# Strassen-Winograd products in the feed-forward part of an adaLN transformer block, with its normalised rows transposed through DRAM

## The chip, the cores and the metric

The kernel runs on 1 core of one Trainium2 chip. The metric is device time in microseconds (us): the median over executions of one kernel. A profiled execution also gives a span, from its first to its last recorded instruction; the timer reads 1.7 to 1.8 us more than the span of the same execution.

In what follows PE is TensorE (matmuls), VectorE is DVE, ScalarE is ACT, GpSimd is POOL, and SP is the engine whose queue issues most loads.

## The reference

A block of a conditioned transformer on x of 2048 tokens by D = 1024, all in bf16. Six modulation rows come from `c` and `w_mod`. A linear-attention half with its own projection `wo` comes first; the change leaves it alone except for its last stretch. Then comes a gated feed-forward part (FFN) with F = 3584:

```python
h = _layernorm(x, axis=-1) * (1 + ca) + sa
x = x + ga * _A_ref(h, A_wqkv, A_wo)                 # linear attention, then @ wo
h = _layernorm(x, axis=-1) * (1 + cb) + sb           # LN2
x = x + gb * ((_gelu(h @ w_gate) * (h @ w_up)) @ w_down)   # 1024 -> 3584 -> 1024
```

## The kernel before

The tokens are handled in 4 groups of 512 (`TG`). The residual x stays in SBUF, the core's on-chip memory (`xres`). The attention half ends with the products by `Wo`; there each finished 128x512 tile in PSUM, the memory that the matmuls write (`psw`, two buffers), is scaled, added to `xres`, and LN2 follows. LN2 transposes its rows on PE:

```python
def wo_proj(tg, oT):
    for tl in range(TT):
        for half in range(NHD):
            psw = psWO.tile([P, NW], FP32, name="psw", tag="wo")      # psWO has bufs=2
            for g in range(KD):
                nc.tensor.matmul(psw[:], lhsT=oT[:, g, tl * P:(tl + 1) * P],
                                 rhs=Wo_sb[:, g, half * NW:(half + 1) * NW], ...)
            gated_residual_update(psw, xres[tt], half, garow)         # two VectorE instructions

def ln_finish(tg, xhs, hT, opc, scol0, ps_pool, pstag):
    for tl, xh in enumerate(xhs):
        psxh = ps_pool.tile([P, D], BF16, name="psxh", tag=pstag)
        for kd in range(KD):
            nc.tensor.transpose(psxh[:, kd * P:(kd + 1) * P], xh[:, kd * P:(kd + 1) * P], ident[:])
        nc.scalar.activation(out=hT[:, :, tl * P:(tl + 1) * P], in_=psxh..., func=AF.Copy)
    # ... scale and shift on VectorE
```

The FFN runs group by group. Every 128 columns of F take 8 matmuls for the gate, 8 for up, and a chain of five instructions on ScalarE and VectorE that makes the gelu and the product. The down product then takes 8 tiles of 28 matmuls:

```python
for jf ...:                                             # 28 per group of tokens
    for k in range(KD): nc.tensor.matmul(psg[:], lhsT=wg_t[...], rhs=h2T[:, k, :], ...)
    for k in range(KD): nc.tensor.matmul(psu[:], lhsT=wu_t[...], rhs=h2T[:, k, :], ...)
    nc.scalar.activation(out=tsq[:], in_=psg[:], func=AF.Square, scale=SQRT_A)
    nc.vector.scalar_tensor_tensor(out=w[:], in0=tsq[:], scalar=1.0, in1=psg[:], ...)
    nc.scalar.activation(out=s[:], in_=w[:], func=AF.Sigmoid, scale=SIG_SCALE)
    nc.vector.tensor_tensor(out=gl[:], in0=s[:], in1=psg[:], op=ALU.mult)
    nc.vector.tensor_tensor(out=actT[:, jf, :], in0=gl[:], in1=psu[:], op=ALU.mult)
...
for tl ...:
    for half ...:
        for jf in range(JF): nc.tensor.matmul(psdn[:], lhsT=actT[...], rhs=wd_sb[...], ...)
        gated_residual_update(psdn, xres[tt], half, gbrow)
```

A tile allocated with a `tag` from a pool takes turns with the other tiles of that tag over the pool's `bufs` buffers; a new tile waits until the old one in its buffer is done with. The framework's scheduler decides in which order each engine gets its instructions, from the program's order and priorities.

## Time and profile before

| | before |
|---|---|
| median, 16 runs | 889.22 us (887.97 to 892.59) |
| span of the profiled execution | 887.5 us |
| PE busy | 97% |
| VectorE, ScalarE busy | 59%, 33% |
| FFN matmuls (gate, up, down) | 2688 |

The page of the profile gives the busy time of each engine (share of the span, number of instructions), the chain of work that ended last by engine, and the costliest groups of instructions (line, engine, operation, output and inputs, shapes, count; then busy us, mean ns of one; then idle time before them).

```profile
PE 859.2 (97%) x4224; PEld 397.7 (45%) x4224; DVE 522.2 (59%) x1015; ACT 294.7 (33%) x518; POOL 3.4 (0%) x27
PE 79%; DVE 10%; DMA 4%; ACT 2%; issue 2%; SPq 1%; ACTq 0%
L409 PE MATMUL psg<-h2T,wg_t 128*128 128x512 bf16 x896 | 211.8, 379 | 0.6 <-DVE gl L423 0.6
L413 PE MATMUL psu<-h2T,wu_t 128*128 128x512 bf16 x896 | 211.7, 379 | 0.0
L432 PE MATMUL psdn<-wd_sb,actT 128*128 128x512 bf16 x896 | 194.9, 379 | 0.0
L424 DVE TENSOR_TENSOR actT<-gl,psu 128x512 bf16<-128x512 bf16 x112 | 77.0, 687 | 12.6 <-DVE gl L423 1.4
```

PE is the limit, and it hardly waits: 0.6 us of idle time in front of 2688 FFN matmuls. The mean of 379 ns is the duration of one matmul in the pipeline, not its price; the price is the distance between starts. PE's timeline gives that (start us, duration us, then the group). In the next fence, 8 psu matmuls start at 832.89 and the next group starts at 834.62, so 8 cost 1.73 us, and one costs 216 ns.

```profile
831.16 1.89 PE L409 MATMUL psg<-h2T,wg_t 128*128 128x512 bf16 x8
832.89 1.89 PE L413 MATMUL psu<-h2T,wu_t 128*128 128x512 bf16 x8
834.62 48.51 PE L432 MATMUL psdn<-wd_sb,actT 128*128 128x512 bf16 x224
```

The next fence is the view by windows of the same kernel: first the Wo stretch, then the FFN. Each line has start:end, the length, then the busy time of PE, weight loads, VectorE, ScalarE and GpSimd with instruction counts in brackets, PE's granted clock, the busy share of the DMA engines, and GB/s.

```profile
222.86:299.16 76.30, 73.72 (x374) 33.33 (x373) 73.50 (x158) 43.11 (x86) 0.00 (x0) 1.00 0.18 56
299.16:883.10 583.94, 583.15 (x2746) 265.86 (x2744) 275.90 (x427) 150.61 (x240) 0.00 (x0) 1.00 0.35 113
```

In the Wo stretch both PE and VectorE are busy for nearly all of the 76 us. In the FFN stretch VectorE is busy for less than half. The 2681 FFN matmuls in this stretch (7 had run earlier) at 215.8 ns are 578.6 us of its 583.9 us. Another 3.6 us are 64 of the LN2 transposes. 16 of them begin at 299.16, and the next matmul at 300.05.

```profile
299.16 1.06 PE L207 MATMUL psxh<-ident,xh 128*128 128x128 bf16 x16
300.05 0.38 PE L409 MATMUL psg<-h2T,wg_t 128*128 128x512 bf16 x1
```

So the FFN has about 1.8 us of idle time and hardly any slack: to shorten it, PE must be given less to do.

### The profile page before, as it was taken

What the parts mean: (1) busy time and instruction counts of PE and PEld (TensorE: products, weight loads), DVE (VectorE), ACT (ScalarE), POOL (GpSimd) and SP (SyncE); (2) the same over time, 40 slices, a digit from 0 to 9 for tenths busy, and PEclk for the clock granted to TensorE, in tenths of its full rate; (3) what the DMA queues carried; (4) which work ended last, traced back from release to release, by engine and by line L of the source; (5) the groups of instructions that cost most, each with busy time, mean ns of one, the idle gap of its engine ahead of it and who ended that gap; (6) DMA issues with size and microseconds to landing.
All of it is one profiled execution on the core that took longest, in us unless ns stands there. A gap on an engine that the chain in (4) does not pass through costs nothing.

```text
span 887.5 us, 10672 instructions
## 1 busy us (share of the span) xinstructions
PE 859.2 (97%) x4224; PEld 397.7 (45%) x4224; DVE 522.2 (59%) x1015; ACT 294.7 (33%) x518; POOL 3.4 (0%) x27
## 2 busy tenths in 40 slices
PE   5898999999999999999999999999999999999998
PEld 3354444444444444444444444444444444444443
DVE  5699978657899865562255655225656214565411
ACT  3255362527665433340023333003333002333200
POOL 0000000000000000000000000000000000000000
PEclk9999999999999999999999999999999999999999
DMA  9944044020500493541033544003544301453000
GB/s 307 353 111 96 1 96 95 13 84 0 190 1 1 159 347 113 187 141 63 24 97 108 186 144 142 24 24 103 182 151 134 107 24 54 149 181 105 1 24 24
DMA packets 107954, 96.37 MB, mean 109 GB/s; under 512 B 34560, under 2 KB 96000, under 8 KB 107904
## 3 DMA queue, kind: packets, MB, share of 16 engines
q1 hardware_dynamic: 105600, 91.49, 33.1%
q10 hardware_dynamic: 2304, 4.20, 1.3%
q8 instruction: 33, 0.54, 0.3%
q14 instruction: 17, 0.14, 0.0%
HBM read 83.10 MB, written 4.19 MB: 98 GB/s over the span
## 4 chain that ended last, share of the span: by engine, by line
PE 79%; DVE 10%; DMA 4%; ACT 2%; issue 2%; SPq 1%; ACTq 0%
PE psdn L432 21%; PE psg L409 21%; PE psu L413 21%; PE pskv L268 8%; PE psq L300 3%; DVE bnst L180 2%; DMA wmt<-in_w_mod_dram 2%; PE psw L351 2%; DMA wqkv<-in_A_wqkv_dram 2%; DVE rt L342 1%; DVE wmt L157 1%; SPq L134 1%; DVE xres L343 1%; PE kvzps L280 1%; DVE xh L195 1%
## 5 line engine op out<-in xcount | busy, mean ns | idle before, releaser
L409 PE MATMUL psg<-h2T,wg_t 128*128 128x512 bf16 x896 | 211.8, 379 | 0.6 <-DVE gl L423 0.6
L413 PE MATMUL psu<-h2T,wu_t 128*128 128x512 bf16 x896 | 211.7, 379 | 0.0
L432 PE MATMUL psdn<-wd_sb,actT 128*128 128x512 bf16 x896 | 194.9, 379 | 0.0
L416 ACT ACTIVATE tsq<-psg 128x512 bf16<-128x512 f32 x112 | 66.8, 597 | 300.9 <-PE psg L409 300.2
L409 PEld LDWEIGHTS <-wg_t 128*128 128x128 bf16 x896 | 87.7, 98 | 106.1 <-issue 0.8
L413 PEld LDWEIGHTS <-wu_t 128*128 128x128 bf16 x896 | 87.7, 98 | 105.6
L432 PEld LDWEIGHTS <-actT 128*128 128x128 bf16 x896 | 87.6, 98 | 105.0
L423 DVE TENSOR_TENSOR gl<-gs,psg 128x512 bf16<-128x512 bf16 x112 | 76.9, 687 | 78.7 <-ACT gs L421 78.6
L268 PE MATMUL pskv<-wqkv,h1T 128*128 128x512 bf16 x512 | 118.4, 386 | 3.9 <-DMA wqkv<-in_A_wqkv_dram 3.9
L418 DVE SCALAR_TENSOR_TENSOR gw<-tsq,psg 128x512 bf16<-128x512 bf16 x112 | 77.0, 688 | 66.4 <-ACT tsq L416 66.4
L342 DVE TENSOR_TENSOR rt<-psdn,gbrow 128x512 bf16<-128x512 f32 x32 | 22.1, 692 | 146.4 <-PE psdn L432 146.4
L421 ACT ACTIVATE gs<-gw 128x512 bf16<-128x512 bf16 x112 | 70.5, 630 | 83.9 <-DVE gw L418 83.9
L424 DVE TENSOR_TENSOR actT<-gl,psu 128x512 bf16<-128x512 bf16 x112 | 77.0, 687 | 12.6 <-DVE gl L423 1.4
L268 PEld LDWEIGHTS <-h1T 128*128 128x128 bf16 x512 | 49.6, 99 | 59.9 <-issue 3.5
L351 PE MATMUL psw<-wo_sb,oT 128*128 128x512 bf16 x256 | 61.5, 379 | 0.2 <-DVE rt L342 0.2
L300 PE MATMUL psq<-h1T,wqkv 128*128 128x512 bf16 x256 | 57.8, 379 | 0.0
L180 DVE BATCH_NORM_STATS2 bnst<-xres 128x6 f32<-128x512 bf16 x64 | 41.9, 672 | 5.2 <-DMA xres<-in_A_x_dram 5.1
L221 ACT ACTIVATE phie<-pskv 128x512 bf16<-128x512 f32 x32 | 19.2, 600 | 72.8 <-PE pskv L268 52.2
L157 DVE CUSTOM_DVE_ANT_0 wmt<-wmt,srow 128x1024 bf16<-128x1024 bf16 x32 | 39.2, 1226 | 2.4 <-DMA wmt<-in_w_mod_dram 2.4
L351 PEld LDWEIGHTS <-oT 128*128 128x128 bf16 x256 | 24.9, 98 | 32.1 <-issue 4.6
L300 PEld LDWEIGHTS <-wqkv 128*128 128x128 bf16 x256 | 24.7, 98 | 28.3
L224 DVE TENSOR_SCALAR phie<-phie 128x512 bf16<-128x512 bf16 x64 | 18.6, 293 | 18.7 <-ACT phie L221 18.7
(69 smaller groups left out, 465.1 us busy)
## 6 DMA issues: line engine op xcount, KB each, us to landing
wg_t<-in_B_w_gate_dram SPq DMA_DIRECT2D x28, 1024.0 KB, 5.4
wu_t<-in_B_w_up_dram SPq DMA_DIRECT2D x28, 1024.0 KB, 7.4
wd_sb<-in_B_w_down_dram SPq DMA_DIRECT2D x7, 1024.0 KB, 11.2
wqkv<-in_A_wqkv_dram SPq DMA_DIRECT2D x3, 2048.0 KB, 17.4
xres<-in_A_x_dram SPq DMA_DIRECT2D x16, 256.0 KB, 6.4
wmb<-in_w_mod_dram SPq DMA_DIRECT2D x4, 1024.0 KB, 11.3
out_dram<-xres ACTq DMA_DIRECT2D x16, 256.0 KB, 2.0
wo_sb<-in_A_wo_dram SPq DMA_DIRECT2D x1, 2048.0 KB, 8.2
```

Of the source, the lines that this page charges most:

```text
L180: nc.vector.bn_stats(out=stats[:, cb, :], in_=xt[:, cb * BW:(cb + 1) * BW])
L268: nc.tensor.matmul(ps[:], lhsT=h1T[:, k, tl * P:(tl + 1) * P], rhs=Wqkv_sb[:, k, col0:col0 + NW], start=(k == 0), stop=(k == KD - 1))
L300: nc.tensor.matmul(psq[:], lhsT=Wqkv_sb[:, k, jq * P:(jq + 1) * P], rhs=h1T[:, k, :], start=(k == 0), stop=(k == KD - 1))
L351: nc.tensor.matmul(psw[:], lhsT=oT[:, g, tl * P:(tl + 1) * P], rhs=Wo_sb[:, g, half * NW:(half + 1) * NW], start=(g == 0), stop=(g == KD - 1))
L409: nc.tensor.matmul(psg[:], lhsT=wg_t[:, k, jl * P:(jl + 1) * P], rhs=h2T[:, k, :], start=(k == 0), stop=(k == KD - 1))
L413: nc.tensor.matmul(psu[:], lhsT=wu_t[:, k, jl * P:(jl + 1) * P], rhs=h2T[:, k, :], start=(k == 0), stop=(k == KD - 1))
L416: nc.scalar.activation(out=tsq[:], in_=psg[:], func=AF.Square, scale=SQRT_A)
L418: nc.vector.scalar_tensor_tensor(out=w[:], in0=tsq[:], scalar=1.0, in1=psg[:], op0=ALU.add, op1=ALU.mult)
L421: nc.scalar.activation(out=s[:], in_=w[:], func=AF.Sigmoid, scale=SIG_SCALE)
L423: nc.vector.tensor_tensor(out=gl[:], in0=s[:], in1=psg[:], op=ALU.mult)
L424: nc.vector.tensor_tensor(out=actT[:, jf, :], in0=gl[:], in1=psu[:], op=ALU.mult)
L432: nc.tensor.matmul(psdn[:], lhsT=actT[:, jf, tl * P:(tl + 1) * P], rhs=wd_sb[:, jf, half * NW:(half + 1) * NW], start=(jf == 0), stop=(jf ...
```

## The change

The intent is to take an eighth of the matmuls out of the FFN with one level of Strassen-Winograd. A product of 2x2 blocks then takes 7 block products in place of 8, and the price is sums of blocks before and combinations after. The blocks are: two halves of D or F, two halves of a unit's weights, and two token groups of 512, so tokens go in 2 pairs of groups. What comes with it:

- Sums and activations are fp16, beside raw weights in bf16. One unit is 256 columns of F: 1 MB of gate and up weights, 4 sums of them on VectorE, 56 matmuls, 7 combinations on VectorE that read PSUM, 3 products in SBUF. Raw weights and sums of one unit share one buffer of 16 KB per partition, of which there are three.
- The gelu is one ScalarE instruction (`Gelu_apprx_tanh`).
- The sums of `w_down` are made during the first pair's gate/up part, stored to DRAM (`t_scr`), and read back for both down parts.
- LN2's rows (`xh`) and x go to DRAM through GpSimd's queue. The rows are read back transposed by DMA, and x as it is. No PE transposes of LN2 are left. The second pair's LN2 is done late, during the first down part.
- The Wo tiles in PSUM take turns over five buffers in place of two.

The diff, cut to its core:

```diff
-                psw = psWO.tile([P, NW], FP32, name="psw", tag="wo")
+                nb = (tl * NHD + half) % 5
+                psw = (psWO if nb % 2 else psA).tile([P, NW], FP32, name="psw", tag="wo" if nb % 2 else "psA")
...
+            nc.gpsimd.dma_start(out=x2_scr[tt][:], in_=xres[tt][:])
...
+            nc.gpsimd.dma_start(out=xh_scr[g][h][tl * P:(tl + 1) * P, :], in_=xh[:])      # ln2_rows
...
+            nc.sync.dma_start_transpose(out=hr[:, :, h * TG:(h + 1) * TG], in_=xh_scr[g][h][:])
+        # scale and shift 8 slices; then t1 = b12-b11, t2 = b22-t1, t3 = b22-b12, t4 = b21-t2
...
+    w_pool = tc.alloc_tile_pool(name="wstream", bufs=3)
+    def w_unit(i):
+        wt = w_pool.tile([P, 2, 2, KD * 2 * P], BF16, name="wt", tag="w")
+        raw = wt[:, 0].rearrange("p u (k fh f) -> p u k fh f", k=KD, fh=2)
+        sm = wt[:, 1].bitcast(F16).rearrange("p u (s k f) -> p u s k f", s=4, k=KH)
+        for u, wdr in enumerate((B_w_gate, B_w_up)):
+            nc.sync.dma_start(out=wt[:, 0, u]..., in_=wdr[:, i * 2 * P:(i + 1) * 2 * P]...)
+        nc.vector.tensor_tensor(out=s1, in0=a21, in1=a22, op=ALU.add)
+        nc.vector.tensor_tensor(out=s2, in0=s1, in1=a11, op=ALU.subtract)
+        nc.vector.tensor_tensor(out=s3, in0=a11, in1=a21, op=ALU.subtract)
+        nc.vector.tensor_tensor(out=s4, in0=a12, in1=s2, op=ALU.subtract)
...
+        for i in range(NPR):                       # 14 units per pair of token groups
+            if i + 1 < NPR:
+                w_cur = w_unit(i + 1)
+            # a12*b21 -> comb "11"; s2*t2 onto pa -> u2; s1*t1 -> pc; s3*t3 onto pa -> comb "22";
+            # a11*b11 of the NEXT unit; a22*t4 onto pa -> product; s4*b22 onto pc -> comb "12"
+            if g == 0:
+                wd_sums(i)                         # load, 4 sums, 4 stores to t_scr on the sync queue
...
+    # down_out: 7 operands, each one tile of w_pool: raw quarters of w_down or t_scr[j], 56 matmuls each
+            nc.scalar.dma_start(out=o_dram[tt * P:(tt + 1) * P, cs], in_=xt[:])
```

In this code a product "onto" a PSUM tile accumulates there. That gives a combination without an instruction, but a copy of the tile by ScalarE (`p1`, `u2`, `u3`) has to be done in between.

## The prediction

> **What bounds the kernel.** TensorE. The page's busy row gives PE 97% of an 887.5 us span, VectorE 59%, ScalarE 33%. The chain of waits puts 63% on the three FFN lines (psg, psu, psdn). There 8 psg or psu matmuls take 1.73 us and 224 psdn matmuls take 48.36 us: 216 ns per 128x512 matmul, the warm interval (215.7 ns) of the Trainium skill, "TensorE: Matmul & The Clock Gate", section "Wait — 56ns, not 53.3ns?"; this trace agrees. The FFN is 2688 of them, 580 us. PE's timeline shows it nearly gap-free from 299 us to 883.1 us, then a 4.4 us tail.
>
> **What the change does.** It runs the FFN products as Strassen-Winograd, 7 half-size products in place of 8.
> - Removed: gate/up 1792 to 1568 matmuls, down 896 to 784. 336 x 216 ns = 72.6 us of PE. Also 128 PE transposes of LN2 (16 take about 1.06 us, so 8 us) and their ScalarE copies, most in the Wo stretch, where the chain names VectorE most.
> - Added on VectorE, per unit of 256 columns (56 matmuls, 12.1 us of PE): 7 PSUM combinations, 3 SBUF products, 4 weight sums of 1024 elements, and 4 w_down sums of 512 in the first half. The trace's 128x512 tensor_tensor takes 687 ns reading PSUM, 419 ns all in 16-bit SBUF; back to back in the chain they step by about 0.60 and 0.33 us. Estimate from these: 7 x 0.60 + 3 x 0.33 + 4 x 0.60 = 7.6 us, 8.9 us with w_down, under 12.1. The sums must run at two elements per cycle (Trainium skill, "VectorE: DVE Perf Modes", "The perf-mode tier table"; 419 against 687 ns agrees).
> - ScalarE: 10 instructions of about 0.6 us, 6 us per unit.
> - DMA: gate/up weights are read twice, not four times; w_down sums go through DRAM; each operand of 1.8 MB has 12.1 us of matmuls to hide in (Wo's 2 MB landed in 8.2 us).
> - LN2 goes through DRAM and two transposing DMAs (2 MB took 9.7 us before), which should land during Wo's third group.
>
> **On the critical path.** All PE savings are. The risk is queue order: VectorE does the sums of unit i+2 ahead of the "22" combination of unit i, and their buffer frees only when unit i-1 ends. From there load (1 MB; estimate 6 us, from 5.4 us before), sums and combination must be done within about 10.4 us. I expect it to hold barely in the second half, and to stall a few us in some units of the first, where scratch stores stand ahead of loads in the sync queue.
>
> **Sum.** FFN starts at 289 us; 2352 x 216 ns = 508; stalls: start 3, first gate/up 10, second 3, down phases 6; tail 5; timer against span 2: about 824 us. Range 803 to 853. Faster by over 2%: 0.94, within: 0.04, slower: 0.02.
>
> **What would show it.** 2352 FFN matmuls at 216 ns; PE idle in the FFN some 20 us, put down to VectorE in the first gate/up; wt sums about 0.7 us each; first FFN matmul near 289 us.
>
> **What would make it wrong.** Weight sums at one element per cycle (1.2 us), or loads landing in 9 us or more: then every unit stalls 2 to 4 us and 50 us or more is lost. Mixed fp16 and bf16 matmuls running slower. Late transposes holding VectorE during Wo. No stalls at all: 800.

## The result and the profile after

| | before | after |
|---|---|---|
| median | 889.22 us (16 runs) | 819.22 us (8 runs, 817.83 to 822.69) |
| span of the profiled execution | 887.5 us | 816.1 us |
| PE busy | 859.2 us, 97% | 780.5 us, 96% |
| VectorE busy | 522.2 us, 59% | 588.1 us, 72% |
| FFN matmuls | 2688 | 2352 |

The ratio is 0.9211, with a 95% interval from 0.9196 to 0.9226: 7.9% faster. The prediction of 824 us was 5 us too high, and the range and the class held.

Here is the page of the kernel after, with the lines that answer to those above: busy row, chain by engine, two of the matmul groups, the weight sums, and one of the weight loads (KB each, median us from issue to landing).

```profile
PE 780.5 (96%) x3760; PEld 357.5 (44%) x3760; DVE 588.1 (72%) x1167; ACT 309.8 (38%) x560; POOL 21.2 (3%) x59
PE 59%; DVE 15%; DMA 15%; issue 6%; SPq 3%; ACT 1%; POOL 1%; POOLq 0%; ACTq 0%; DVEq 0%
L484 PE MATMUL psa<-h2t,wt 128*128 128x512 f16 x448 | 107.5, 383 | 2.9 <-ACT p L448 2.9
L484 PE MATMUL psb<-h2r,wt 128*128 128x512 f16 x448 | 102.2, 379 | 4.5 <-DVE c L512 2.1
L476 DVE TENSOR_TENSOR wt<-wt 128x1024 f16<-128x1024 bf16 x28 | 19.4, 694 | 60.1 <-DMA wt<-in_B_w_up_dram 54.3
wt<-in_B_w_up_dram SPq DMA_DIRECT2D x28, 512.0 KB, 5.5
```

Three things are to be seen. The chain has gone from 79% PE to 59%, with VectorE and DMA at 15% each: PE is still 96% busy, but the path that ended last now runs through the weight loads as well. A weight sum of 1024 elements takes 694 ns, as hoped for. And the first sum of each unit sat waiting for the load of `w_up`, for 54.3 us in all. Whether that wait costs anything is not in this line, because VectorE is not the limit; the experiments answer it.

The view by windows of the kernel after: the Wo stretch, then the first pair's gate/up, its down, and the second pair's gate/up and down.

```profile
222.14:291.40 69.26, 67.09 (x303) 29.28 (x302) 66.37 (x132) 32.74 (x66) 12.49 (x22) 1.00 0.57 159
291.40:465.39 173.99, 170.90 (x785) 76.64 (x786) 135.34 (x256) 80.33 (x140) 1.08 (x2) 1.00 0.62 187
465.39:551.30 85.91, 85.08 (x393) 38.35 (x392) 56.79 (x96) 8.37 (x13) 4.26 (x8) 1.00 0.70 224
551.30:726.78 175.48, 171.16 (x785) 77.05 (x784) 119.49 (x201) 81.93 (x140) 0.00 (x0) 0.99 0.36 102
726.78:811.50 84.72, 84.72 (x393) 38.28 (x391) 37.06 (x54) 5.41 (x9) 0.00 (x0) 1.00 0.43 148
```

A gate/up part has 784 matmuls, 169.2 us at 215.8 ns; a down part has 392, 84.6 us. So the four stretches carry 4.8, 1.3, 6.3 and 0.1 us over their matmuls. In the first gate/up the excess is spread in small pieces. In the second it is one place, at its very start, on PE's timeline (in brackets: idle time before, and what ended it):

```profile
551.30 1.89 PE L484 MATMUL psa<-h2r,wt 128*128 128x512 f16 x8
553.03 1.03 PE L484 MATMUL psb<-h2r,wt 128*128 128x512 f16 x4
555.47 1.02 PE L484 MATMUL psb<-h2r,wt 128*128 128x512 f16 x4 [1.41 <-DVE yt L579]
559.39 3.52 PE L484 MATMUL psa<-h2t,wt 128*128 128x512 f16 x8 [2.91 <-ACT p L448]
562.75 1.89 PE L484 MATMUL psb<-h2t,wt 128*128 128x512 f16 x8
```

PE waits twice, 4.3 us together, and the next 8 matmuls then take 3.52 us where 8 others take 1.89: PE had fallen to about half its clock (the view by windows gives a granted clock of 0.53 from 559.2 to 562.8 us, and 1.00 before and after), and that cost 1.6 us more. VectorE's timeline over the same time says why the first wait was there:

```profile
552.92 0.69 DVE L476 TENSOR_TENSOR wt<-wt 128x1024 f16<-128x1024 bf16 x1 [4.47 <-DMA wt<-in_B_w_up_dram]
553.53 0.68 DVE L478 TENSOR_TENSOR wt<-wt 128x1024 f16<-128x1024 bf16 x1
554.13 0.68 DVE L477 TENSOR_TENSOR wt<-wt 128x1024 f16<-128x1024 f16 x1
554.73 0.68 DVE L579 TENSOR_TENSOR yt<-psb,w 128x512 f16<-128x512 f32 x1
```

The last tiles of the first down part were ready in PSUM, and PE waited for their buffers. But the instruction that empties them (`yt`, L579) stood in VectorE's queue behind the weight sums of the second unit, and these had stood for 4.47 us waiting for their load. VectorE takes its queue in order: the Trainium skill, "TensorE: Matmul & The Clock Gate", section "Architectural detail: the array is 16× 32×32, not 1× 128×128", calls ACT and DVE strict FIFO queues, and this trace agrees. The sync queue's own timeline shows that the load could be issued only at 546.4 and 546.9 us. Ahead of it stood the reads of x for the down part, which held the queue for 6.64 us:

```profile
539.70 6.64 SPq L574 DMA_DIRECT2D xio<-x2s  x4
546.39 0.43 SPq L471 DMA_DIRECT2D wt<-in_B_w_gate_dram  x1
546.87 0.65 SPq L471 DMA_DIRECT2D wt<-in_B_w_up_dram  x1
```

These reads were held up themselves: there are six buffers for x (`xio`), and a read waits until the output store of an earlier tile has left its buffer. In the whole kernel the sync queue waited 85.3 us for such stores, in 22 waits (view of waits: queue and line, what it waited for; us in all, times, longest). Much of this harms nothing; here a weight load stood behind it. More buffers for x, or another queue for its reads, would go at this link of the chain; neither was tried.

```profile
SPq L574 <- DMA out_dram<-xio: 85.3, 22, 9.7
```

In the middle of the second gate/up the same order does no harm, as the VectorE line and the PE line below show. There VectorE waits 2.98 us for the load, makes four sums, and then does the combinations. These are finished at 629.7 us, just before PE begins at 630.09 us the group of matmuls that needs them, without a wait.

```profile
625.91 0.69 DVE L476 TENSOR_TENSOR wt<-wt 128x1024 f16<-128x1024 bf16 x1 [2.98 <-DMA wt<-in_B_w_up_dram]
628.45 1.28 DVE L512 TENSOR_TENSOR c<-psb,u 128x512 f16<-128x512 f32 x2
```
```profile
630.09 3.62 PE L484 MATMUL psb<-h2r,wt 128*128 128x512 f16 x16
```

**The account of the 71.4 us of span.** The time before the Wo stretch gave 0.7 us, the Wo stretch 7.0 us (76.30 against 69.26), and the FFN stretch 63.8 us (583.94 against 520.10); the tail after the last matmul took 0.2 us back (4.4 against 4.6). The FFN's 63.8 us are 329 matmuls fewer in that stretch (71.0 us) and 64 transposes fewer (3.6 us), less 10.7 us of new idle time: 12.5 us now against 1.8 us. The Wo stretch's 7.0 us are 7 FFN matmuls (1.5 us) and 64 transposes fewer (3.9 us by the distance between starts), and 1.6 us that were not taken apart.

### The profile page after: what moved, and what is told of

It reads as the page before. It is cut to its first block, busy times and chain, and to the rows that moved or that the text cites. A ratio compares the mean times of both kernels' runs of the same rounds, so it can differ in the third digit from the quotient of the medians.

```text
span 816.1 us, 10358 instructions
## 1 busy us (share of the span) xinstructions
PE 780.5 (96%) x3760; PEld 357.5 (44%) x3760; DVE 588.1 (72%) x1167; ACT 309.8 (38%) x560; POOL 21.2 (3%) x59
## 4 chain that ended last, share of the span: by engine, by line
PE 59%; DVE 15%; DMA 15%; issue 6%; SPq 3%; ACT 1%; POOL 1%; POOLq 0%; ACTq 0%; DVEq 0%
PE psa L484 18%; PE psb L484 14%; PE pskv L267 8%; PE psa L567 7%; DMA wt<-in_B_w_up_dram 5%; PE psb L567 4%; PE psq L299 3%; DMA wmt<-in_w_mod_dram 2%; PE psw L360 2%; DMA wqkv<-in_A_wqkv_dram 2%; DVE bnst L179 2%; DVE wmt L156 1%; DMA xhs<-xl 1%; DVE bnst L390 1%; SPq L133 1%
## 5 line engine op out<-in xcount | busy, mean ns | idle before, releaser
L484 PEld LDWEIGHTS <-wt 128*128 128x128 f16 (+1 forms) x1568 | 153.6, 98 | 196.9 <-issue 13.2
L484 PE MATMUL psa<-h2t,wt 128*128 128x512 f16 x448 | 107.5, 383 | 2.9 <-ACT p L448 2.9
L484 PE MATMUL psb<-h2r,wt 128*128 128x512 f16 x448 | 102.2, 379 | 4.5 <-DVE c L512 2.1
L484 PE MATMUL psa<-h2r,wt 128*128 128x512 f16 x448 | 101.6, 379 | 1.0 <-ACT u L448 0.9
L567 PEld LDWEIGHTS <-A 128*128 128x128 f16 x672 | 65.8, 98 | 80.6 <-issue 1.7
L567 PE MATMUL psa<-wd,A 128*128 128x512 f16 (+1 forms) x448 | 97.8, 379 | 0.8 <-DVE yt L579 0.7
L507 ACT ACTIVATE gl<-c 128x512 f16<-128x512 f16 x84 | 52.9, 630 | 111.0 <-DVE c L512 111.0
L448 ACT ACTIVATE u<-psa 128x512 f32<-128x512 f32 x112 | 65.7, 595 | 59.7 <-PE psa L484 59.0
L512 DVE TENSOR_TENSOR c<-psb,u 128x512 f16<-128x512 f32 x112 | 74.4, 686 | 17.9 <-ACT u L448 15.4
L448 ACT ACTIVATE p<-psa 128x512 f32<-128x512 f32 x64 | 37.0, 589 | 104.2 <-DMA out_dram<-xio 56.3
L476 DVE TENSOR_TENSOR wt<-wt 128x1024 f16<-128x1024 bf16 x28 | 19.4, 694 | 60.1 <-DMA wt<-in_B_w_up_dram 54.3
L484 PE MATMUL psb<-h2t,wt 128*128 128x512 f16 x224 | 52.9, 379 | 0.0
```

What stands on the lines that cost most here:

```text
L448: nc.scalar.activation(out=t[:], in_=ps[:], func=AF.Copy)
L476: nc.vector.tensor_tensor(out=s1, in0=a21, in1=a22, op=ALU.add)
L484: nc.tensor.matmul(ps[:], lhsT=a[:, u, k, :], rhs=b[:, k, :], start=(start and k == 0), stop=(k == KH - 1), skip_group_check=True)
L507: nc.scalar.activation(out=t[:], in_=src, func=AF.Gelu_apprx_tanh)
L512: nc.vector.tensor_tensor(out=t[:], in0=ps[:], in1=sb[:], op=ALU.add)
L567: nc.tensor.matmul(ps[:], lhsT=a[:, i, q * P:(q + 1) * P], rhs=b[:, i, :], start=(start and i == 0), stop=(i == NPR - 1), skip_group_check ...
```

## The experiments

The theory was that the new idle time comes from VectorE's queue order. The sums of a coming unit stand ahead of combinations that PE needs at once, and their load can begin only when a whole unit's buffer, raw weights and sums together, comes free, and when the sync queue has dealt with what stands before it. Rivals were: the w_down scratch traffic on the sync queue, the output stores in ScalarE's queue, and, for the Wo stretch, which of two parts of the change brought the 7 us. Ten kernels were run, all with right results. The labels are only names.

| run | median us | ratio to before (95%) | span us |
|---|---|---|---|
| changed kernel | 819.22 | 0.9211 (0.9196 to 0.9226) | 816.1 |
| e1_down8 | 829.82 | 0.9333 (0.9321 to 0.9346) | 829.2 |
| e10_buf2 | 817.76 | 0.9194 (0.9181 to 0.9208) | 816.8 |
| e4_raw4 | 810.59 | 0.9128 (0.9113 to 0.9143) | 807.3 |
| e11_down8_raw4 | 829.89 | 0.9329 (0.9314 to 0.9344) | 826.1 |
| e5_outq | 823.51 | 0.9255 (0.9235 to 0.9276) | 819.4 |
| e6_raw4_tsq | 814.47 | 0.9159 (0.9145 to 0.9174) | 813.5 |
| e7_wo2 | 823.46 | 0.9267 (0.9248 to 0.9286) | 824.5 |
| e8_before_rot | 889.99 | 1.0012 (0.9995 to 1.0029) | 887.9 |
| e9_ln2dma | 895.25 | 1.0070 (1.0055 to 1.0085) | 893.2 |
| e13_ln2dma_rot | 895.97 | 1.0073 (1.0053 to 1.0092) | 894.4 |

### e1_down8: the down products in 8 again

From the changed kernel: the down part made of plain products, without w_down sums, scratch or combinations. Gate/up is untouched.

```diff
-            if g == 0:
-                wd_sums(i)
...
-        # seven operands: wd_v quarters and t_scr[0..3], combinations between them
+        for nh in range(2):
+            wd = operand(wd_v[0][:, :, nhs])
+            for th, a in enumerate((A11, A21)):
+                for q in range(TT): mm_f(ps, a, q, wd, True)
+            wd = operand(wd_v[1][:, :, nhs])
+            for th, a in enumerate((A12, A22)):
+                for q in range(TT):
+                    mm_f(acc[th * TT + q], a, q, wd, False)
+                    finish(th * TT + q, nh, acc[th * TT + q], None)
```

> Only gate/up keep 7 products; the down projection runs all 8 half-size products, and the w_down sums and their stores to DRAM are gone. Theory (TensorE bounds, so every matmul not run is worth its 216 ns and the additions are hidden): 112 more matmuls cost 24.2 us, less up to 4.8 us of PE idle of the first gate/up half that the w_down sums may cause: about 839 to 843 us. Rival (the gain came from halved weight reads or from the LN2 path, and the down part's savings are eaten by its operand loads and combinations): the time stays within 5 us of the changed kernel's 819.

Measured: 829.82 us, only 10.6 us slower than the changed kernel, though it runs 112 matmuls more, which are 24.2 us. That lies between the two expectations and fits neither: the cost is far less than the matmuls, and more than 5 us. The windows of its four FFN stretches say where the rest lies:

```profile
292.70:462.15 169.45, 169.37 (x785) 76.70 (x786) 115.87 (x199) 82.30 (x140) 1.08 (x2) 1.00 0.39 111
462.15:558.84 96.69, 96.22 (x440) 43.84 (x448) 43.92 (x84) 3.71 (x5) 4.26 (x8) 1.00 0.50 143
558.84:728.05 169.21, 169.21 (x785) 76.70 (x784) 110.91 (x188) 82.14 (x140) 0.00 (x0) 1.00 0.35 99
728.05:824.75 96.70, 96.22 (x440) 43.77 (x447) 17.91 (x33) 0.63 (x1) 0.00 (x0) 1.00 0.22 72
```

Both gate/up stretches are 169.2 to 169.5 us: all of the idle time in gate/up is gone. So the idle time in the changed kernel's gate/up, 4.8 and 6.3 us, is brought by the Strassen form of the down part: by the w_down sums with their loads and stores in the first half, and by the down part's late instructions and loads at the start of the second. In that kernel the down part's Strassen form returns less than half of what it takes out. The view of waits also warns against a tempting number (engine, tile and line, what it waited for; us in all, times, longest):

```profile
DVE wt L476 <- DMA wt<-in_B_w_up_dram: 71.0, 25, 6.5
```

VectorE waited 71.0 us for weight loads here, more than the 54.3 us of the changed kernel, and gate/up had no idle time at all. The wait does harm only where something urgent is queued behind it.

### e10_buf2: two weight buffers in place of three

```diff
-    w_pool = tc.alloc_tile_pool(name="wstream", bufs=3)
+    w_pool = tc.alloc_tile_pool(name="wstream", bufs=2)
```

> Weight buffers 2 instead of 3. Theory (the third buffer buys nothing in the loop, because VectorE takes the sums of unit i+2 as soon as their buffer frees and stands in front of the combination of unit i either way; the window from a unit's end to the combination is what counts): 815 to 826 us, gate/up stretches within 5 us of before. Rival (prefetch depth hides the loads; with two buffers each unit waits for its 5.3 us load): 28 units lose 3 us or more, 900 us or above.

Measured: 817.76 us, as fast as with three, as the theory expected. Its stretches took 174.7, 91.6, 169.2 and 84.6 us: the idle time at the start of the second gate/up is gone, and 5 us of waits for operands in the first down part came in its place. VectorE's order at the passage is the same as in the changed kernel, sums first and the emptying of the last tiles behind them; but PE reached its last down tiles so much later (558.35 us for the first gate/up matmul, against 551.30) that the tiles were emptied in time. So the third buffer of 16 KB buys nothing. A shortage of buffers as such is not the trouble; a fourth buffer of this kind could not be tried, as it doesn't fit in SBUF.

### e4_raw4: raw weights and sums in separate buffers

The same 48 KB, cut otherwise: four buffers for raw weights (8 KB each) and two for sums. The loads no longer wait for a buffer in which sums are still being read. The down operands go in two halves, so as to fit.

```diff
-        wt = w_pool.tile([P, 2, 2, KD * 2 * P], BF16, name="wt", tag="w")
-        raw = wt[:, 0].rearrange(...)
-        sm = wt[:, 1].bitcast(F16).rearrange(...)
+        wt = w_pool.tile([P, 2, KD * 2 * P], BF16, name="wt", tag="wr", bufs=4)
+        ws = w_pool.tile([P, 2, KD * 2 * P], F16, name="ws", tag="ws", bufs=2)
+        raw = wt[:].rearrange(...)
+        sm = ws[:].rearrange(...)
...
-            wt = w_pool.tile([P, NPR, NW], src.dtype, name="wd", tag="w")
-            nc.sync.dma_start(out=wt[:], in_=src)
+            for c, tag in enumerate(("wr", "ws")):
+                wt = w_pool.tile([P, NC, NW], src.dtype, name="wd" + tag, tag=tag, bufs=2 if c else 4)
+                nc.sync.dma_start(out=wt[:], in_=src[:, c * NC:(c + 1) * NC, :])
```

> Same memory, cut otherwise: raw weights in 4 buffers of 8 KB, sums in 2, so that sums can only be made one unit ahead and never meet a load still in flight. Theory (queue order: combinations wait behind sums that wait for a load): VectorE's waits for weight loads, 54 us in all in the changed kernel, fall under 10 us, PE's idle in the first gate/up (174.0 us for 169.2 us of matmuls) falls from 4.8 to under 2 us, total 3 to 5 us less: 814 to 817. Rival (the idle there comes from VectorE's or DMA's amount of work with the w_down sums): no change, 818 to 820.

Measured: 810.59 us (809.05 to 813.43), 8.6 us faster than the changed kernel by the medians (7.4 by the ratios), and the fastest of all the kernels here. The gain was larger than expected. It came in another place, too: of the first gate/up's 4.8 us, 2.9 us were left where under 2 were expected. The windows of its four FFN stretches:

```profile
290.92:463.03 172.11, 170.09 (x784) 76.67 (x785) 135.37 (x256) 80.20 (x140) 1.08 (x2) 1.00 0.61 184
463.03:548.71 85.68, 84.67 (x388) 38.33 (x392) 60.14 (x102) 8.37 (x13) 4.25 (x8) 1.00 0.81 246
548.71:717.92 169.21, 169.21 (x785) 76.71 (x784) 116.86 (x195) 82.53 (x140) 0.00 (x0) 1.00 0.34 95
717.92:802.69 84.77, 84.51 (x388) 38.24 (x391) 37.05 (x54) 5.41 (x9) 0.00 (x0) 1.00 0.44 146
```

The second gate/up is down to its bare matmuls (169.21 us, from 175.48), and the first has lost 1.9 us. The excess over matmul time in the FFN fell from 12.5 to 4.2 us. VectorE's wait for weight loads, 54.3 us before, no longer appears in its list of waits. VectorE's timeline at the start of the second gate/up:

```profile
548.91 0.69 DVE L583 TENSOR_TENSOR yt<-psb,w 128x512 f16<-128x512 f32 x1 [1.41 <-PE psb L571]
549.52 0.68 DVE L477 TENSOR_TENSOR ws<-wt 128x1024 f16<-128x1024 bf16 x1
```

The tile is emptied within a moment of PE's finishing it, and the first sum of the second unit comes after it with no wait for its load. This is the main evidence for the theory. It does not separate the two effects of the cut: loads that are issued earlier, and sums that stand later in VectorE's queue because their buffers come free later. Both are there: the second unit's `up` load was issued 7.6 us before the second gate/up began (541.10 against 548.71 us), in the changed kernel only 4.4 us before (546.87 against 551.30), and its first sum now stands behind the emptying of the tile. In the first gate/up 2.9 us are left, and VectorE now waits there 8.3 us in all for the loads of w_down; whether these cause the 2.9 us stays open (see e6_raw4_tsq).

### e11_down8_raw4: both edits together

> Plain 8-product down, gate/up with 7, weights in the 4 raw and 2 sum buffers of the earlier run. Without w_down sums the gate/up stretches had no idle in the 3-buffer version already (169.45 and 169.05 us against 169.2 us of matmuls), so the recut should buy nothing here: 828 to 831, and the down part's 112 matmuls are then worth 18 to 21 us against the recut kernel's 810.6. Rival (the recut helps by something else, such as earlier operand loads): 822 to 825.

Measured: 829.89 us, the same as e1_down8 without the recut. So the recut's gain is the taking away of idle time that the Strassen down part had brought, and the halved operands cost nothing that shows. It also prices that down part anew: with the recut it is worth 829.89 − 810.59 = 19.3 us of its 24.2 by the medians (17.9 by the ratios, as the two ran on different chips), where it had been worth 10.6.

### e5_outq: the output stores on another queue

The second wait at 559 us is named as one for ScalarE (`p`). ScalarE's timeline puts 56.3 us of idle time before that copy, ended by `out_dram<-xio`, the last of the output stores in ScalarE's queue. It is one single wait, and for most of it, during the down part, ScalarE had no copy to make. The theory in this test was that these stores hold ScalarE up.

```diff
-            nc.scalar.dma_start(out=o_dram[tt * P:(tt + 1) * P, cs], in_=xt[:])
+            nc.gpsimd.dma_start(out=o_dram[tt * P:(tt + 1) * P, cs], in_=xt[:])
```

> Output DMAs issued from the GpSimd queue instead of ScalarE's. Theory (ScalarE's FIFO is held by output DMAs waiting for VectorE when the second half starts, so the first two copies of the second gate/up come late and PE idles 2.9 us): that idle goes, 816 to 817.5 us. Rival (VectorE, which has finishing work and sums queued there, is what is late; ScalarE only shows it): the PE idle of 4.3 us at the start of the second half stays, now put down to VectorE, 818 to 820 us.

Measured: 823.51 us (819.94 to 825.2), 4.3 us slower (3.9 by the ratios), so the gain that the theory expected did not come. The stores had held the copy up: it began 7.45 us after the second gate/up's first matmul in the changed kernel (558.75 against 551.30 us), and 1.06 us after it here (553.66 against 552.60 us).

```profile
558.75 0.60 ACT L448 ACTIVATE p<-psa 128x512 f32<-128x512 f32 x1 [56.30 <-DMA out_dram<-xio]
553.66 0.60 ACT L448 ACTIVATE p<-psa 128x512 f32<-128x512 f32 x1 [51.67 <-PE psa L484]
```

But PE's idle time there stayed about as it was (1.56 and 2.35 us, now for ScalarE's `u` and VectorE's `c`), because VectorE waited as long for the weight load as before (4.93 us) and made its combinations as late. In these two waits PE did not fall to half its clock, and the second gate/up took 173.5 us in place of 175.5. The first down part took 1.8 us more, with 2.4 us of new idle time, and the tail after the last matmul grew by 4.0 us, to 8.6. VectorE's last line in this kernel is

```profile
812.04 0.42 DVE L581 TENSOR_TENSOR xio<-yt,xio 128x512 bf16<-128x512 f16 x1
```

and the span ends at 819.4 us, 6.9 us later; in the changed kernel it ended 2.9 us after the same instruction. The median landing of such a store was 2.1 us against 1.9, so the landing alone doesn't account for the tail; what fills the rest is not in the trace. So the stores in ScalarE's queue were a link of the chain and not its cause: they waited because VectorE was late, and without them PE waits for VectorE all the same.

### e6_raw4_tsq: the scratch stores off the sync queue

From e4_raw4: the stores of the w_down sums go through GpSimd's queue, to keep them out of the way of the loads on the sync queue.

```diff
-            nc.sync.dma_start(out=t_scr[j][:, i, :], in_=t[:, j, :])
+            nc.gpsimd.dma_start(out=t_scr[j][:, i, :], in_=t[:, j, :])
```

> The recut kernel (4 raw, 2 sum buffers; 810.6 us) with the stores of the w_down sums moved from the sync queue to the GpSimd queue. There the first gate/up half still takes 172.1 us for 169.2 us of matmuls, and VectorE waits 8.3 us in all for w_down loads that stand in the sync queue behind such stores. Theory (queue order): those waits fall under 3 us, the stretch to about 170, total 808 to 810. Rival (amount of VectorE or DMA work in that half): no change, 810 to 812; worse if GpSimd's slower issue holds the two sum buffers.

Measured: 814.47 us, 3.9 us slower than e4_raw4 by the medians (2.8 by the ratios; the chips differ). The move does not pay. The stores landed in 4.8 us (median) in place of 3.0. The sums' two buffers (`tws`) so came free later, VectorE waited for them, and PE for VectorE's combinations (view of waits):

```profile
DVE tws L459 <- DMA ts<-tws: 14.1, 8, 2.7
PE psb L485 <- DVE c L513: 7.7, 5, 3.0
```

The first gate/up grew from 172.1 to 180.0 us. It is the same mechanism with another trigger: a sum that waits in VectorE's queue delays a combination that PE needs. VectorE's waits for w_down loads did go, from 8.3 us to none in its list, as the theory had it; the new waits cost more. An issue also took longer on GpSimd's queue (0.54 us against a median of 0.37). So this run does not tell what the scratch stores cost on the sync queue, nor what the 2.9 us in e4_raw4's first gate/up come from.

### e7_wo2: two PSUM buffers for Wo in the changed kernel

```diff
-                nb = (tl * NHD + half) % 5
-                psw = (psWO if nb % 2 else psA).tile([P, NW], FP32, name="psw", tag="wo" if nb % 2 else "psA")
+                psw = psWO.tile([P, NW], FP32, name="psw", tag="wo")
```

> The changed kernel with Wo's PSUM tiles back in one pool of 2 buffers, as before the change. The stretch from the first Wo matmul to the first FFN matmul went from 76.3 us to 69.3 us. Theory (that came from PE transposes gone, about 5 us, and less VectorE work there): within 2 us of the changed kernel, 818 to 821 us. Rival (it came from the five PSUM buffers): the stretch goes back to 75 us or so, 824 us or more.

Measured: 823.46 us, 4.2 us slower than the changed kernel (5.0 by the ratios), so the five buffers count there; that is nearly what the rival had expected. Its Wo stretch by windows:

```profile
222.90:299.30 76.40, 72.77 (x321) 31.03 (x319) 71.84 (x141) 33.85 (x67) 13.06 (x23) 1.00 0.51 148
```

16 FFN matmuls had slipped in between the Wo tiles here, which are 3.5 us; without them the stretch is 72.9 us against 69.3 in the changed kernel and, without its 7, 74.8 in the kernel before. (The profiled run was the slowest of the four, 826.24 us; another 3 us of its difference lie in the first gate/up.) What the five buffers do is to be read on VectorE's timeline of the changed kernel: between 276.7 and 285.8 us it prepares the transposed rows (scale, shift and the four sums t1 to t4) and empties one Wo tile in all that time. PE ran 45 Wo matmuls, more than five tiles of 8, from 275.77 us on before it had to wait, and then only for 1.22 us.

### e8_before_rot: the five buffers in the kernel before

The same two lines, put into the kernel before.

> The kernel before with only the change's rotation of Wo's PSUM tiles over five buffers. Theory (transposes and VectorE work are what Wo pays for): within 2 us of before, 887 to 890. Rival (PSUM buffers): 882 to 884.

Measured: 889.99 us, ratio 1.0012 with an interval that includes 1: nothing gained. In that kernel PE waited 0.2 us for Wo tiles in the whole stretch, so there was nothing to gain.

### e9_ln2dma: LN2 through DRAM in the kernel before

Alone, without Strassen: rows to DRAM on GpSimd's queue, read back by a transposing DMA, no PE transposes.

```diff
-        h2_tiles[tg] = ln_finish(tg, ln_xhat(tg, ln2_stats.pop(tg), xh2_pool), h2T, opcB, 3 * KD,
-                                 ps_pool, pstag)
+        for tl, xh in enumerate(ln_xhat(tg, ln2_stats.pop(tg), xh2_pool)):
+            nc.gpsimd.dma_start(out=xh_scr[tg][tl * P:(tl + 1) * P, :], in_=xh[:])
+        nc.sync.dma_start_transpose(out=h2T[:], in_=xh_scr[tg][:])
+        # scale and shift on VectorE as before
```

> The kernel before with LN2's rows stored to DRAM and read back by transposing DMAs for all four groups, plain FFN. Theory: 128 PE transposes (8 us by their spacing, half in Wo, half between the FFN's groups) and the ScalarE copies go and nothing else changes: 881 to 885. Rival (the DRAM round trip is late, and PE waits for the first h2T): 888 or more, with an idle of PE ahead of the first psg.

Measured: 895.25 us, 5.9 us slower than before, though 128 transposes (7.4 us of PE by the distance between starts) are gone. PE's and VectorE's timelines show the largest piece:

```profile
313.44 3.57 PE L417 MATMUL psg<-h2T,wg_t 128*128 128x512 bf16 x8 [5.67 <-DVE gl L431]
```
```profile
312.25 0.55 DVE L195 TENSOR_SCALAR xh<-xres,bnmv,rstd 128x1024 bf16<-128x1024 bf16 x1 [3.41 <-DMA xhs<-xh]
```

The rows of a later token group waited 3.41 us in VectorE's queue for a row buffer that was being stored. The gelu chain of the FFN's first tiles stood behind them, and PE was idle for 5.67 us and then ran at half its clock. It is again VectorE's order, in another place.

### e13_ln2dma_rot: LN2 through DRAM and five buffers

> The kernel before with both of the change's parts outside the FFN products: LN2 through DRAM, and Wo's PSUM tiles over five buffers. Each alone gained nothing (895 and 890 us against 889). Theory (the LN2 path holds VectorE for several us at a time, and five buffers let PE run on meanwhile, as taking them out of the changed kernel cost 4 us): at least 4 us better than with two buffers, 885 to 891. Rival (LN2 rows of groups 2 and 3 waiting for their stores are what costs, after Wo): 893 to 896, no gain from the buffers.

Measured: 895.97 us, no better than without the five buffers. PE was idle for 8.34 us in front of the same group (`xh` had waited 5.29 us for the stores). So in the kernel before neither of the two parts pays, nor both together. In the changed kernel the row path runs with the second pair's rows put off until the first down part, which these two experiments do not have; whether late rows would make the path pay in the kernel before was not tried.

## Why the prediction was right, and where its steps failed

The total was right: 824 us predicted, 819.22 us measured. The terms as written add up to 826 us; it was rounded to about 824. Term by term, for the profiled execution:

| term | predicted us | measured us |
|---|---|---|
| FFN starts, with the stall at the start | 289 + 3 | 291.4 |
| 2352 FFN matmuls | 508 | 507.6 |
| stalls, first gate/up | 10 | 4.8 |
| stalls, second gate/up | 3 | 6.3 |
| stalls, down parts | 6 | 1.4 |
| tail | 5 | 4.6 |
| timer against span | 2 | 1.7 |

**What held.** PE was the limit, and a matmul with fp16 beside bf16 operands costs what a bf16 one does (8 in 1.73 us). The sums ran at twice the rate of a tensor_tensor that reads PSUM, as hoped for: 0.69 us for 1024 elements, against 0.687 us for 512 before. The load of an `up` half landed in 5.5 us (predicted 6). PE's idle time in the FFN's first gate/up was put down mostly to VectorE, as announced (3.0 us of waits, 0.9 of them for a Wo tile; another 0.9 us were for ScalarE), and inside the loop of the second half the order did hold barely (e.g. combinations done at 629.7, needed at 630.09).

**"On the critical path. All PE savings are."** This step failed in size. PE was freed of 72.5 us of matmuls and 7.4 us of transposes, 79.9 us together, and the span fell by 71.4 us. The 10.7 us of idle time that the change brought into the FFN are more than the difference (other stretches gave some back), and they were not a fixed cost of the scheme: e4_raw4 gets 8.6 us back (7.4 by the ratios) with the same sums and matmuls in the same memory. The loss in gate/up goes with one part: e1_down8 shows that the Strassen form of the down products, 24.2 us of matmuls, was worth 10.6 us.

**The stalls: terms mis-sized.** The prediction put 19 us of stalls into the FFN after its start, and 12.5 us were measured. The first gate/up and the down parts were put too high, by 5.2 and 4.6 us. The second gate/up was put too low (3 for 6.3), and its idle time was all in a place that the prediction did not look at: not the loop, whose order it had worked out, but the passage from the first down part into the second gate/up, where x's reads hold the weight load back and the sums hold the last tiles back. The errors had opposite signs, so the total looks better than its parts. The half clock after the two waits (1.6 us) was not in the sum at all.

**"Queue order" was the right risk.** The mechanism named there, sums of a coming unit ahead of combinations of the present one, was the one that cost. e4_raw4 confirms it by taking the load wait away, and e6_raw4_tsq and e9_ln2dma by making the same kind of wait elsewhere. The prediction linked it to the buffer of unit i−1, which suggests more buffers; e10_buf2 shows that one fewer does no harm, and one more did not fit. That scratch stores ahead of loads are what stalls the first half, as the prediction had it, is not shown: e6_raw4_tsq moved them and brought in a larger cost.

**"Also 128 PE transposes of LN2."** The transposes did go, and the Wo stretch shrank by 7.0 us, of which 3.9 us are transposes and 1.5 us FFN matmuls that no longer ran in it. But the step took the LN2 path to be a gain by itself. Alone in the kernel before it costs 5.9 us (e9_ln2dma), and in the changed kernel 4.2 us of the gain hang on five PSUM buffers (e7_wo2), which the prediction did not mention.

**What stays open.** The changed kernel's runs spread over 5 us and single spans by as much, so differences of 1 to 2 us between kernels (e10_buf2 against the changed kernel) are not claimed. What fills the last 4 us of e5_outq's tail, and which of the recut's two effects counts, was not settled. No run took gate/up alone back to 8 products: that its 224 matmuls fewer (48.3 us) are worth their price is read from the traces, not from an experiment of its own.

## What to carry to other kernels

When a change trades PE work for VectorE work, VectorE's busy share says little; find each instruction that PE is about to need and see what stands ahead of it in the same queue, above all an instruction that waits for a load. Buffers that hold a load and what is computed from it together tie the next load to the last reader of the results; with separate buffers, same memory, the load went out earlier and 8.6 us came back here (7.4 by the ratios). Cost the passages between stages separately from the loops, and test the parts of a bundled change apart: here one part paid 10.6 of the 24.2 us it was credited with, and another was a loss on its own.

## What the Trainium skill lacked or had wrong

- "TensorE: Matmul & The Clock Gate", section "What's actually happening", puts the half clock after at least one idle window of about 3.4 us. Here it came after an idle time of 2.91 us (one of 1.41 us and 4 matmuls lay before it): 8 matmuls took 3.52 us where 8 others took 1.89; in e7_wo2 8 took 3.57 us after 2.90 us. Waits of 5.67 and 8.34 us gave 3.57 us each, which agrees with the page.
- The same page gives 215.7 ns for a warm matmul of 512 columns, which agrees (8 in 1.73 us), but doesn't say what mixed operands do: fp16 beside bf16 ran at the same 1.73 us per 8.
- No page was found that gives the size of VectorE's overlap: in a row, sums recorded at 0.69 us started 0.60 us apart, so their recorded duration is longer than their price.
- "DMA: Bandwidth & Descriptors", section "Issuing engine by pattern", says that queues of sync and scalar are generally faster than GpSimd's. The traces agree and put a size on it: stores of 128 KB landed in 4.8 us against 3.0 (e6_raw4_tsq), and with the output on GpSimd's queue the span ended 6.9 us after the last VectorE instruction in place of 2.9 (e5_outq). No page has such a tail.
- No page was found that treats this: one waiting instruction in VectorE's in-order queue delays unrelated combinations behind it. The page on TensorE says that the queue is strict FIFO, not what follows from that for the placing of prefetched sums; separating the buffers so that the wait went away brought 8.6 us of 819 here (7.4 by the ratios).
